# Delta-rule attention, Mish MoE and Sinkhorn MoE in one kernel: block 1's triangular inverses split between VectorE and TensorE

## The chip, the cores and the metric

One core of one Trainium2 chip runs the whole kernel. The metric is device time of one execution, in microseconds. The engines are called PE (TensorE matmul), PEld (TensorE weight load), DVE (VectorE), ACT (ScalarE), POOL (GpSimd) and SP (the queue that issues DMAs).

## What is computed

```python
def _attn_ref(q, k, v, beta):                      # 4 x 8 heads, 768 tokens, head size 48
    k_n = k / (np.linalg.norm(k, axis=-1, keepdims=True) + 1e-06)
    state = np.zeros((B, H, D, D), dtype=np.float32)
    for t in range(S):
        y[:, :, t] = np.einsum('bhd,bhde->bhe', q[:, :, t], state)
        v_old = np.einsum('bhde,bhd->bhe', state, kt)
        state = state + bt[:, :, :, None] * np.einsum('bhd,bhe->bhde', kt, vt - v_old)

def _moe_ref(x, w_in, w_out):                      # 3072 tokens, 384 -> 2048 -> 384
    h = x @ w_in
    sp = np.where(h > 20.0, h, np.log1p(np.exp(np.minimum(h, 20.0))))
    return (h * np.tanh(sp)) @ w_out

def _moe2_ref(x, w_gate, w1, w2):                  # 8 experts, 384 -> 1024 -> 384
    P = np.exp(logits - logits.max())              # then 8 rounds of row and column scaling
    for e in range(E):
        out += P[:, e:e + 1] * (np.maximum(x @ w1[e], 0.0) @ w2[e])
```

## The kernel before

The 768 tokens are cut into six blocks, c = 0 to 5, of two chunks of 64 tokens. The recurrence of a chunk becomes a 64x64 triangular inverse per head. Each inverse is made from its two 32x32 diagonal triangles: DVE inverts those by elimination, all 128 triangles of a block at once, in a tile called lane that holds one triangle per partition and 32-row group; then PE joins two 32x32 triangles to 64x64. The steps for one block are: lane_in_one (L1101, a DVE transpose of the masked Gram matrices gx into lane, and a memset of the diagonal); elim_ops (30 elimination steps, each a product at L1114 and an addition at L1120); st_lane_out (L1129 and L1130, two DVE transposes into t11 and diag); st_m1 (L1157) and st_m2 (L1172), the joining matmuls of 32x32 with evacuations between them; then st_z, st_w, st_s and st_y, the chunk's own small matmuls. diag_left (L1092, ACT) copies the lower diagonal blocks to the left ahead of lane_in_one.

While that runs, PE works through the first MoE of block c: for each of U1 = 16 slices of the hidden layer m_first (L308, nine matmuls 128x512) and, two slices later, m_second (L1341, nine matmuls). They are split in three passes of high and low parts. The order is written by hand: marks s0 to s15 are the 16 steps, f1 to f4 follow them while the last m_second drain, and s16 to s23 are the eight slices of one expert of the second MoE (e_first L308, y0_second L332), which only blocks 0 and 1 run here. Tables attach the attention work of the next block to marks: what is in pe runs as matmul stages at that mark, what is in rest is called there, and each engine executes its own instructions strictly in that written order.

Block 0 differs from the later blocks: the weights of the first MoE arrive for the first time, as 64-bit numbers. Per step, ACT makes L193 and L206, DVE makes L196 and L201 (decoding the slice used two steps later), ACT rounds it to the high part (L251), and DVE subtracts for the low part (L270), after which SP stores the slice (L279) and fetches the slice four further on (L170, L174). ACT also does Mish (L1320) and the high part of the result (L1328), and DVE its low part (L1330). m_first of a step needs L251 and L270 of that slice. Into what is left of DVE's step, fill(us) puts elimination operations of block 1's inverse from a queue eq, by an assumed cost; drain_elim empties the queue.

In block 0, block 1's diag_left stands at s1 and s2, lane_in_one at s3, eliminations from s4 on, and at s17 the rest of the eliminations, the two transposes, and POOL's work for block 1. At s18, array_kept (L1567) issues eight matmuls 128x512 whose result nothing reads, then st_m1 follows, at s19 st_z, the first half of st_m2, and st_w, and so on to s22. Small matmul stages take a PSUM bank from bank().

Of the kernel before, what the change touches and what calls it, by code (L numbers as in the profile page):

```python
# [8 lines left out]
F32 = mybir.dt.float32  # L9
# [4 lines left out]
AF = mybir.ActivationFunctionType  # L14
ALU = mybir.AluOpType
AX = mybir.AxisListType
# [69 lines left out]
def delta_mish_sinkhorn_kernel(  # L86
# [740 lines left out]
    if True:  # L827
# [6 lines left out]
        gxs = [ap_p.tile([128, 4, H, CH], F32, name=f"gx{i}") for i in range(2)]  # L834
        nrms = [[ap_p.tile([128, 4 * H], F32, name=f"{n}{i}") for n in ("ss", "ne", "rn", "bn")] for i in range(2)]
        us = [[ap_p.tile([128, 2, DM], F32, name=f"us{g}{i}") for i in range(2)] for g in range(NG)]
        lane = ap_p.tile([128, 32, 32], F32, name="lane")
        t11 = ap_p.tile([128, 32, 32], F32, name="t11")
        yd = ap_p.tile([128, 4, DM], F32, name="yd")
        diag = yd.rearrange("p t d -> p (t d)")[:, 0:1024].rearrange("p (b i) -> p b i", i=32)  # L840
# [265 lines left out]
        def elim_ops(c):  # L1106
            ops = []
            for s in range(1, 31):
                n = 31 - s
                slot = [None]  # L1110

                def prod(s=s, n=n, slot=slot):
                    slot[0] = t11.rearrange("p b i -> p (b i)")[:, 0:n * s].rearrange("p (n s) -> p n s", s=s)
                    nc.vector.tensor_tensor(  # L1114
                        out=slot[0], in0=lane[:, s + 1:32, s:s + 1].to_broadcast([128, n, s]),
                        in1=lane[:, s:s + 1, 0:s].to_broadcast([128, n, s]), op=ALU.mult,
                    )
# [8 lines left out]
            return ops  # L1126

        def st_lane_out(c):
            nc.vector.transpose(out=t11.rearrange("p b i -> p i b"), in_=lane.rearrange("p t i -> p i t"))  # L1129
            nc.vector.transpose(out=diag.rearrange("p b i -> p i b"), in_=lane)  # L1130
# [259 lines left out]
        if True:  # L1390
# [146 lines left out]
            warm(2)  # L1537
            rounded(1)
            in1 = [op for _, op in lane_in_one(1)]
            ops1 = deque(elim_ops(1))  # L1540

        NU = U1 + U2
        MARKS = [f"s{f}" for f in range(U1)] + ["f1", "f2", "f3", "f4"] + [f"s{f}" for f in range(U1, NU)]
# [17 lines left out]

        carry = []

        def array_kept():
            ps = bank()
            for _ in range(8):
                mm(ps, lhsT=x1h[:, 0, 0:128], rhs=x1h[:, 0, :], start=True, stop=True)  # L1567

        def window(c):

            pe = {m: [] for m in MARKS}
# [10 lines left out]
            if c == 0:  # L1582
                for t in (2, 3):
                    pe["s2"].append(lambda t=t: st_s(0, t))
                for t in range(4):
                    rest[f"s{1 + t // 2}"].append(lambda t=t: diag_left(1, t))
                rest["s3"].append(lambda: [op() for op in in1])
                rest["s3"].append(lambda: eq.extend(ops1))
            if nxt < NBLK:
                m0, at = PLACES[c][0:2]  # L1590
                rest[MARKS[m0]].append(drain_elim)
                if c == 0:
                    rest[MARKS[m0]].append(lambda: nc.vector.memset(seed_sb, 0.0))
                rest[MARKS[m0]].append(lambda: st_lane_out(nxt))
                if c == 0:
# [8 lines left out]
                    for m, names in ((22, "--m"), (23, "zMw"), (24, "Nsy"), (25, "ZWS"), (26, "Y"), (27, "-")):  # L1604
                        for x in names:
                            at += [m, m]
                            if x == "-":
                                ch += [lambda: lambda: None] * 2
                            elif x == "m":
                                ch += [lambda hf=hf: (hf or array_kept(), m_run(st_m1(nxt, hf))[0])[1] for hf in range(2)]  # L1610
# [47 lines left out]
        if True:  # L1658
            banks[:] = [0, [A1, A1]]
            for c in range(NBLK):  # L1660
# [44 lines left out]
                for f in range(U1 + (3 if c < NE0 else 2)):  # L1705
# [39 lines left out]
                        decodes(min(U1, f + 3))  # L1745
                        begins(min(U1, f + 4))
                    if not c:
                        fill((2.0 + 1.2, 0.7, 0.0)[f - U1] if f >= U1 else 0.0 if f == 3 else 1.0)
                    elif c < NE0:
                        fill(2.9 if f < U1 else 2.0 if f < U1 + 2 else 0.5)  # L1750
                    else:
                        fill(2.6)
# [218 lines left out]
```

## Time and profile before

| | us |
|---|---|
| median of 3 runs | 2167.09 |
| lowest, highest | 2166.68, 2168.41 |
| the profiled execution | 2170.71 |
| its span, first to last instruction | 2168.9 |
| PE busy in it | 2144.8 |
| DVE, ACT, POOL busy | 1394.2, 712.9, 629.9 |
| mean granted TensorE clock, as a share of full | 0.993 |

Times in rows are counted from the first instruction of the span. Block 0's 16 steps run from about 64 us to 143 us, marks f1 to s23 of block 0 to about 220 us. The other 1950 us hold blocks 1 to 5, which the change leaves as they are, and the rest of the second MoE.

### The profile page before, as it was taken

What the parts mean: (1) busy time and instruction counts of PE and PEld (TensorE: products, weight loads), DVE (VectorE), ACT (ScalarE), POOL (GpSimd) and SP (SyncE); (2) the same over time, 40 slices, a digit from 0 to 9 for tenths busy, and PEclk for the clock granted to TensorE, in tenths of its full rate; (3) what the DMA queues carried; (4) which work ended last, traced back from release to release, by engine and by line L of the source; (5) the groups of instructions that cost most, each with busy time, mean ns of one, the idle gap of its engine ahead of it and who ended that gap; (6) DMA issues with size and microseconds to landing.
All of it is one profiled execution on the core that took longest, in us unless ns stands there. A gap on an engine that the chain in (4) does not pass through costs nothing.

```text
span 2168.9 us, 35002 instructions
## 1 busy us (share of the span) xinstructions
PE 2144.8 (99%) x14118; PEld 1771.2 (82%) x14118; DVE 1394.2 (64%) x2316; ACT 712.9 (33%) x1332; POOL 629.9 (29%) x489
## 2 busy tenths in 40 slices
PE   8999999999999999999999999999999999999999
PEld 6778878888888888888888888888888888888887
DVE  7893846566413576776777776666666666666665
ACT  7772533343334443333333311112122211121222
POOL 4214241544224466768787400001000000000000
PEclk8999999999999999999999999999999999999999
DMA  6676636463447257655545344544444354534441
GB/s 190 233 295 221 210 119 195 135 210 129 151 167 251 88 196 262 210 198 196 212 173 211 116 156 136 186 138 149 157 151 141 131 160 145 166 133 159 156 154 44
DMA packets 148993, 370.37 MB, mean 171 GB/s; under 512 B 36832, under 2 KB 76576, under 8 KB 148576
## 3 DMA queue, kind: packets, MB, share of 16 engines
q1 hardware_dynamic: 148256, 367.75, 50.2%
q8 instruction: 111, 1.82, 0.3%
q10 hardware_dynamic: 576, 0.39, 0.1%
q14 instruction: 50, 0.41, 0.1%
HBM read 274.15 MB, written 93.95 MB: 170 GB/s over the span
## 4 chain that ended last, share of the span: by engine, by line
PE 93%; DVE 3%; ACT 2%; DMA 1%; issue 1%; SPq 0%; POOL 0%; DVEq 0%; ACTq 0%
PE s L680 34%; PE b L613 32%; PE psh L308 9%; PE x L1341 8%; PE psa L1051 2%; PE y L332 1%; PE psa L1221 1%; DMA kq<-in_w_out_dram 1%; PE psa L1255 1%; PE psa L1199 1%; PE psa L1239 1%; PE psa L1172 1%; PE psa L1362 0%; PE psa L1157 0%; ACT sq L950 0%
## 5 line engine op out<-in xcount | busy, mean ns | idle before, releaser
L613 PE MATMUL b<-gx,gw 128*128 128x512 f32 x3036 | 793.5, 389 | 0.1
L620 DVE TENSOR_TENSOR gt<-b,gt 128x512 f32<-128x512 f32 x644 | 436.1, 689 | 425.8 <-PE b L613 407.6
L613 PEld LDWEIGHTS b<-gx,gw 128*128 128x128 f32 x3036 | 569.4, 188 | 119.0 <-ACT gt L622 0.8
L680 PE MATMUL s<-gh,gw 128*128 128x512 f32 x2208 | 622.4, 390 | 0.2 <-ACT gf L710 0.2
L655 ACT ACTIVATE gh<-gt 128x512 fp32r<-128x512 f32 x368 | 232.8, 633 | 942.0 <-DVE gt L649 939.6
L680 PEld LDWEIGHTS s<-gh,gw 128*128 128x128 f32 x2208 | 413.7, 188 | 86.1 <-ACT gf L710 0.8
L680 PE MATMUL s<-gl,gw 128*128 128x512 f32 x1104 | 326.7, 390 | 0.0
L649 DVE SCALAR_TENSOR_TENSOR gt<-gt,gp 128x512 f32<-128x512 f32 x336 | 277.8, 827 | 4.5
L308 PE MATMUL psh<-x,w 128*128 128x512 f32 x1008 | 263.3, 405 | 5.9 <-ACT w L251 2.5
L680 PEld LDWEIGHTS s<-gl,gw 128*128 128x128 f32 x1104 | 206.8, 188 | 42.7
L308 PEld LDWEIGHTS psh<-x,w 128*128 128x128 f32 x1008 | 187.1, 191 | 53.6 <-DVE w L270 7.6
L658 POOL TENSOR_TENSOR gl<-gt,gh 128x512 fp32r<-128x512 f32 x128 | 185.9, 1458 | 86.3 <-ACT gh L655 78.2
L658 DVE TENSOR_TENSOR gl<-gt,gh 128x512 fp32r<-128x512 f32 x240 | 164.6, 686 | 36.3 <-ACT gh L655 36.0
L553 POOL TENSOR_TENSOR gx<-gxr,gx 128x768 fp32r<-128x768 f32 x18 | 34.9, 1940 | 413.1 <-ACT gx L552 413.1
L1341 PE MATMUL x<-gh,w 128*128 128x512 f32 x576 | 150.2, 396 | 0.1
L475 POOL TENSOR_TENSOR gw<-gr,gw 128x640 fp32r<-128x640 f32 x70 | 117.5, 1681 | 83.4 <-ACT gw L494 83.4
L1330 POOL TENSOR_TENSOR gl<-x,gh 128x512 fp32r<-128x512 f32 x55 | 70.8, 1288 | 223.2 <-ACT gh L1328 214.8
L1341 PEld LDWEIGHTS x<-gh,w 128*128 128x128 f32 x576 | 105.9, 188 | 23.3 <-issue 1.4
L1322 ACT ACTIVATE x<-psh 128x512 f32<-128x512 f32 x80 | 47.7, 596 | 119.2 <-PE psh L308 114.9
L1015 POOL TENSOR_TENSOR kq<-kq,mask_sb 64x256 f32<-64x256 f32 (+1 forms) x80 | 68.3, 854 | 48.6 <-ACT kq L1010 44.4
L1341 PE MATMUL x<-gl,w 128*128 128x512 f32 x288 | 81.0, 389 | 0.0
L475 POOL TENSOR_TENSOR gw<-raw,gw 128x384 fp32r<-128x384 f32 x70 | 74.4, 1083 | 7.3 <-ACT gw L516 7.3
(208 smaller groups left out, 1953.9 us busy)
## 6 DMA issues: line engine op xcount, KB each, us to landing
gw<-wg SPq DMA_DIRECT2D x57, 1280.0 KB, 8.1
w<-wd SPq DMA_DIRECT2D x88, 768.0 KB, 4.5
gw<-wg SPq DMA_DIRECT2D x57, 768.0 KB, 5.1
wg<-gw SPq DMA_DIRECT2D x29, 1280.0 KB, 6.2
wg<-gw SPq DMA_DIRECT2D x29, 768.0 KB, 5.2
wd<-w SPq DMA_DIRECT2D x24, 768.0 KB, 6.9
gr<-in_w_dram SPq DMA_DIRECT2D x35, 384.0 KB, 3.3
raw<-in_w_dram SPq DMA_DIRECT2D x35, 384.0 KB, 3.8
```

Source lines behind the costliest of these rows:

```text
L308: mm(ps, lhsT=wi(u, pw, kc), rhs=(xh, xl)[px][:, kc, :], start=(n == 0), stop=(n == 3 * KD - 1))
L475: nc.gpsimd.tensor_tensor(out=w[:, 1, lo:hi], in0=r, in1=w[:, 0, lo:hi].bitcast(F32), op=ALU.subtract)
L613: mm(ps, lhsT=w[:, pw, i * 128:i * 128 + 128], rhs=x[:, px, j, :], start=(n == 0), stop=(n == last))
L620: add = lambda o, i: nc.vector.tensor_tensor(out=t[:, o], in0=ps, in1=t[:, i], op=ALU.add)
L649: nc.vector.scalar_tensor_tensor(out=t, in0=t, scalar=0.0, in1=pbs[u, e][:, o:o + 512], op0=ALU.max, op1=ALU.mult)
L655: nc.scalar.activation(out=h, in_=t, func=AF.Copy)
L658: return lambda: eng.tensor_tensor(out=l, in0=t, in1=h.bitcast(F32), op=ALU.subtract)
L680: mm(o[k], lhsT=w[:, pw, at:at + 128], rhs=hids[s, z][ph], start=(start and new and n == 0), stop=(end and not new and n == 2))
L1015: nc.gpsimd.tensor_tensor(out=o, in0=o, in1=mask_sb[p, None, :].to_broadcast([64, hs.stop - hs.start, CH]), op=ALU.mult)
L1322: nc.scalar.activation(out=mi_x[u % 2], in_=hps.pop(u), func=AF.Mish)
L1330: eng.tensor_tensor(out=l, in0=p, in1=h.bitcast(F32), op=ALU.subtract)
L1341: mm(x2ps[c][k], lhsT=wo(u, pw, k * 128, k * 128 + 128), rhs=(h, l)[pg], start=(f == 0 and n == 0), stop=(f == U1 - 1 and n == 2))
```

## The change

Block 1's inverse alone, the one that is made during block 0, is cut differently. DVE now inverts 16x16 triangles: lane is widened to 1056 columns so that a view lane16 holds both halves of a triangle, and elim16_ops has 14 steps instead of 30, each acting on two halves. PE joins two 16x16 triangles to 32x32 in three stages: st_16a (128 matmuls in two halves at f1 and f2), st_16b (64 matmuls at f4) and st_16c (128 matmuls, half at f4 and half at s16). The evacuations are one ACT operation that also scales by a 0/1 column (lower16), two DVE operations (upper16), and four ACT operations into diag. halves16 makes the two columns once, by two reductions on DVE. diag_left moves from s1 and s2 to one each at s5 to s8, lane_in_one from s3 to s8, and the two transposes of st_lane_out from s17 to s15. The fill times of s3, s16 and s17 change, array_kept is gone. POOL's work for block 1 and st_m1 and all behind it keep their marks.

```diff
+        def elim16_ops():
+            ops = []
+            for s in range(1, 15):
+                n = 15 - s
...
+        def st_16a(hf):
+            if hf == 0:
+                shared16["a"] = bank().rearrange("p (b i) -> p b i", i=16)
+            ps = shared16["a"]
+            for b in range(16 * hf, 16 * hf + 16):
+                for p in range(0, 128, 32):
+                    q = slice(p, p + 16)
+                    mm(ps[p:p + 32, b], lhsT=diag[q, b, :], rhs=t11[q, b, 0:16], start=True, stop=True)
+            return lambda: hf and nc.scalar.activation(out=e16, in_=ps, func=AF.Copy, scale=lower16)
...
+                    mm(ps[q, b], lhsT=diag[q, b, :], rhs=e16[q, b, :], start=True, stop=True)
...
+                    mm(ps[p:p + 16, b], lhsT=e16[q, b, :], rhs=diag[q, b, 16:32], start=True, stop=True)
...
-            ops1 = deque(elim_ops(1))
+            ops1 = deque(elim16_ops())
+            halves16()
...
-        def array_kept():
-            ps = bank()
-            for _ in range(8):
-                mm(ps, lhsT=x1h[:, 0, 0:128], rhs=x1h[:, 0, :], start=True, stop=True)
...
                 for t in range(4):
-                    rest[f"s{1 + t // 2}"].append(lambda t=t: diag_left(1, t))
-                rest["s3"].append(lambda: [op() for op in in1])
-                rest["s3"].append(lambda: eq.extend(ops1))
+                    rest[f"s{5 + t}"].append(lambda t=t: diag_left(1, t))
+                rest["s8"].append(lambda: [op() for op in in1])
+                rest["s8"].append(lambda: eq.extend(ops1))
+                rest["s15"].append(drain_elim)
+                rest["s15"].append(lambda: st_lane_out(1))
+                pe["f1"].append(lambda: st_16a(0))
+                pe["f2"].append(lambda: st_16a(1))
+                pe["f4"] += [st_16b, lambda: st_16c(0)]
+                pe[f"s{U1}"].append(lambda: st_16c(1))
...
-                        fill((2.0 + 1.2, 0.7, 0.0)[f - U1] if f >= U1 else 0.0 if f == 3 else 1.0)
+                        fill((2.0, 0.0, 0.0)[f - U1] if f >= U1 else 1.0)
```

The first place is DVE in the steps, around lane_in_one (STREAM_TRANSPOSE of gx into lane). Before, at steps s3 and s4:

```order
L270 TENSOR_TENSOR w_1157<-kq_138,w_1157 128x768
L1101 STREAM_TRANSPOSE lane<-gx_151 128x1024
L1102 MEMSET lane 128x32
L196 SCALAR_TENSOR_TENSOR kq_139<-kq_139 128x768
L201 SCALAR_TENSOR_TENSOR kq_139<-kq_139 128x768
L1330 TENSOR_TENSOR gl<-psh,gh 128x512
L270 TENSOR_TENSOR w_1284<-kq_139,w_1284 128x768
L196 SCALAR_TENSOR_TENSOR kq_140<-kq_140 128x768
L201 SCALAR_TENSOR_TENSOR kq_140<-kq_140 128x768
L1114 TENSOR_TENSOR t_165<-lane 128x30
L1120 TENSOR_TENSOR lane<-lane,t_165 128x30
```

With the change, DVE at steps s7, s8 and s9 (L1405 is what L1330 was, L1104 what L1101 was; L1140 and L1147 are the new eliminations):

```order
L1405 TENSOR_TENSOR gl<-psh,gh 128x512
L270 TENSOR_TENSOR w_1160<-kq_139,w_1160 128x768
L1104 STREAM_TRANSPOSE lane<-gx_151 128x1024
L1105 MEMSET lane 128x32
L196 SCALAR_TENSOR_TENSOR kq_140<-kq_140 128x768
L201 SCALAR_TENSOR_TENSOR kq_140<-kq_140 128x768
L1140 TENSOR_TENSOR t_167<-lane 128x28
L1147 TENSOR_TENSOR lane<-lane,t_167 128x2x14
L1140 TENSOR_TENSOR t_167<-lane 128x52
L1147 TENSOR_TENSOR lane<-lane,t_167 128x2x13x2
L1140 TENSOR_TENSOR t_167<-lane 128x72
L1405 TENSOR_TENSOR gl<-psh,gh 128x512
```

The transpose into lane moved five steps later, steps s3 to s7 have no elimination work, and the eliminations start right behind the transpose, four or five to a step.

The second place is DVE at the end of the eliminations and the transposes out of lane (STREAM_TRANSPOSE into t and yd). Before, at s17 and s18:

```order
L1114 TENSOR_TENSOR t_165<-lane 128x30
L1120 TENSOR_TENSOR lane<-lane,t_165 128x30
L1593 MEMSET seed_sb 128x1
L1129 STREAM_TRANSPOSE t_165<-lane 128x32x32
L1130 STREAM_TRANSPOSE yd<-lane 128x32x32
L270 TENSOR_TENSOR w_91<-raw,w_91 128x768
L323 SCALAR_TENSOR_TENSOR hl<-psh,hh 128x512
L907 COPY mb_177<-psa 32x512 x2
```

With the change, at s14, s15 and f1 (the w_1161 and w_1280 slices are the first two of the expert):

```order
L1405 TENSOR_TENSOR gl<-psh,gh 128x512
L270 TENSOR_TENSOR w_1160<-kq_141,w_1160 128x768
L1147 TENSOR_TENSOR lane<-lane,t_167 128x2x2x13
L1140 TENSOR_TENSOR t_167<-lane 128x28
L1147 TENSOR_TENSOR lane<-lane,t_167 128x2x14
L270 TENSOR_TENSOR w_1161<-raw,w_1161 128x768
L1405 TENSOR_TENSOR gl<-psh,gh 128x512
L1204 STREAM_TRANSPOSE t_167<-lane 128x32x32
L1205 STREAM_TRANSPOSE yd<-lane 128x32x32
L270 TENSOR_TENSOR w_1280<-raw,w_1280 128x768
L1405 TENSOR_TENSOR gl<-psh,gh 128x512
```

The transposes now stand behind the low part (gl) of slice 14 and ahead of that of slice 15.

The third place is PE between two m_second, here of slices 13 and 14. Before:

```order
L1341 MATMUL x_1248<-gl,w_90 128x512
L1341 MATMUL x_1249<-gl,w_90 128x512
L1341 MATMUL x_1250<-gl,w_90 128x512
L1341 MATMUL x_1248<-gh,w_91 128x512
L1341 MATMUL x_1249<-gh,w_91 128x512
```

With the change, at f1 and f2 (st_16a is L1169 and reads t and yd; L1416 is what L1341 was):

```order
L1416 MATMUL x_1246<-gl,w_90 128x512
L1169 MATMUL psa<-t_167,yd 32x16 x64
L1416 MATMUL x_1244<-gh,w_91 128x512
L1416 MATMUL x_1245<-gh,w_91 128x512
L1416 MATMUL x_1246<-gh,w_91 128x512
L1416 MATMUL x_1244<-gh,w_91 128x512
L1416 MATMUL x_1245<-gh,w_91 128x512
L1416 MATMUL x_1246<-gh,w_91 128x512
L1416 MATMUL x_1244<-gl,w_91 128x512
L1416 MATMUL x_1245<-gl,w_91 128x512
L1416 MATMUL x_1246<-gl,w_91 128x512
L1169 MATMUL psa<-t_167,yd 32x16 x64
```

Between m_second of slice 13 and that of slice 14, PE now has 64 matmuls that need both transposes, and 64 more ahead of m_second of slice 15; st_16b and st_16c (192 matmuls) follow behind that one.

## Rows read from the trace of the kernel before

**Rows 1.** The page, part 4: the chain that ended last, by engine.

```profile
PE 93%; DVE 3%; ACT 2%; DMA 1%; issue 1%; SPq 0%; POOL 0%; DVEq 0%; ACTq 0%
```

**Rows 2.** Busy time by stretch: length, engines' busy us (instructions), clock, DMA share, GB/s.

```profile
100.00:120.00 20.00, 19.83 (x84) 15.16 (x83) 19.39 (x33) 16.30 (x23) 0.00 (x0) 1.00 0.98 362
...
360.00:460.00 100.00, 100.00 (x1212) 82.59 (x1211) 62.96 (x117) 37.82 (x71) 45.72 (x41) 1.00 0.54 172
```

**Rows 3.** Timeline of PE: start, length, engine, line, tiles, shape, count [idle before <-releaser].

```profile
74.00 2.32 PE L308 MATMUL psh<-x,w 128*128 128x512 f32 x9
...
83.10 0.51 PE L308 MATMUL psh<-x,w 128*128 128x512 f32 x1 [0.66 <-ACT w L251]
...
107.45 2.41 PE L308 MATMUL psh<-x,w 128*128 128x512 f32 x9
...
134.31 0.39 PE L308 MATMUL psh<-x,w 128*128 128x512 f32 x1
...
238.81 2.20 PE L308 MATMUL psh<-x,w 128*128 128x512 f32 x9
...
242.89 2.20 PE L308 MATMUL psh<-x,w 128*128 128x512 f32 x9
```

**Rows 4.** Timeline of DVE, one step of block 0.

```profile
101.81 0.69 DVE L1330 TENSOR_TENSOR gl<-psh,gh 128x512 fp32r<-128x512 f32 x1
102.42 0.95 DVE L270 TENSOR_TENSOR w<-kq,w 128x768 fp32r<-128x768 f32 x1
...
105.15 0.32 DVE L1114 TENSOR_TENSOR t<-lane 128x168 f32<-128x168 f32 x1
...
106.15 0.68 DVE L1330 TENSOR_TENSOR gl<-psh,gh 128x512 fp32r<-128x512 f32 x1
```

**Rows 5.** Timeline of DVE: transpose into lane, an elimination, the transposes out.

```profile
83.96 2.05 DVE L1101 STREAM_TRANSPOSE lane<-gx 128x1024 f32<-128x1024 f32 x1
...
96.53 0.27 DVE L1114 TENSOR_TENSOR t<-lane 128x108 f32<-128x108 f32 x1
...
152.89 2.27 DVE L1129 STREAM_TRANSPOSE t<-lane 128x1024 f32<-128x1024 f32 x1
154.98 2.04 DVE L1130 STREAM_TRANSPOSE yd<-lane 128x1024 f32<-128x1024 f32 x1
```

**Rows 6.** Timeline of ACT: diag_left, and the ends of one step.

```profile
71.64 1.70 ACT L1092 ACTIVATE gx<-gx 32x256 f32<-32x256 f32 x4
...
96.38 0.90 ACT L251 ACTIVATE w<-kq 128x768 fp32r<-128x768 f32 x1 [0.88 <-DVE kq L201]
...
99.41 0.60 ACT L1328 ACTIVATE gh<-psh 128x512 fp32r<-128x512 f32 x1
```

**Rows 7.** Timeline of PE behind the 16 steps: s16, array_kept, st_m1, st_z, s19.

```profile
143.32 2.59 PE L308 MATMUL psh<-x,w 128*128 128x512 f32 x9 [0.24 <-ACT x L1348]
...
154.12 2.01 PE L1567 MATMUL psa<-x 128*128 128x512 f32 x8
156.06 2.21 PE L1157 MATMUL psa<-t,gx 32*32 32x32 f32 x128
158.55 0.25 PE L1199 MATMUL psa<-us,kq 48*64 48x48 f32 x1 [0.28 <-ACT mb L1145]
...
160.47 0.23 PE L1199 MATMUL psa<-us,kq 48*64 48x48 f32 x1 [0.79 <-DVE mb L907]
...
161.70 3.71 PE L308 MATMUL psh<-x,w 128*128 128x512 f32 x9
```

**Rows 8.** Busy time by short stretch, columns as in rows 2.

```profile
58.00:60.00 2.00, 2.00 (x72) 1.95 (x68) 1.87 (x5) 1.36 (x3) 1.92 (x3) 1.00 0.00 0
...
66.00:68.00 2.00, 1.00 (x5) 0.51 (x3) 1.04 (x3) 1.07 (x2) 0.00 (x0) 1.00 1.04 326
...
70.00:72.00 2.00, 2.00 (x6) 1.32 (x5) 1.63 (x3) 1.83 (x3) 0.00 (x0) 0.50 1.04 424
...
162.00:163.00 1.00, 1.00 (x3) 0.81 (x3) 0.97 (x3) 0.41 (x1) 1.00 (x1) 0.50 1.07 449
```

More of the change, by code (lines that the diff above doesn't have):

```diff
@@ L836, in delta_mish_sinkhorn_kernel @@
         us = [[ap_p.tile([128, 2, DM], F32, name=f"us{g}{i}") for i in range(2)] for g in range(NG)]
-        lane = ap_p.tile([128, 32, 32], F32, name="lane")
+        lanes = ap_p.tile([128, 1056], F32, name="lane")
+        lane = lanes[:, 0:1024].rearrange("p (t i) -> p t i", i=32)
+        lane16 = lanes.rearrange("p (b x) -> p b x", b=2)[:, :, 0:512].rearrange("p b (t i) -> p b t i", i=32)
+        lower16, upper16 = [ap_p.tile([128, 1], F32, name=f"h{i}") for i in range(2)]
         t11 = ap_p.tile([128, 32, 32], F32, name="t11")
@@ L1126, in elim_ops, with prod, add @@
             return ops
+        def elim16_ops():
+            ops = []
+            for s in range(1, 15):
+                n = 15 - s
+                slot = [None]
+                def prod(s=s, n=n, slot=slot):
+                    v = t11.rearrange("p b i -> p (b i)")[:, 0:2 * n * s]
+                    slot[0] = v.rearrange("p (b n s) -> p b n s", b=2, s=s)
+                    nc.vector.tensor_tensor(
+                        out=slot[0], in0=lane16[:, :, s + 1:16, s:s + 1].to_broadcast([128, 2, n, s]),
+                        in1=lane16[:, :, s:s + 1, 0:s].to_broadcast([128, 2, n, s]), op=ALU.mult,
+                    )
+                def add(s=s, n=n, slot=slot):
+                    o = lane16[:, :, s + 1:16, 0:s]
+                    nc.vector.tensor_tensor(out=o, in0=o, in1=slot[0], op=ALU.add)
+                cost = 0.2 + 2 * n * s / 960.0
+                ops += [(cost, prod), (cost, add)]
+            return ops
@@ new lines, in halves16 @@
+        def halves16():
+            v = id_sb.rearrange("p (q h x) -> p h q x", h=2, x=16)
+            for h, o in ((0, upper16), (1, lower16)):
+                nc.vector.tensor_reduce(out=o, in_=v[:, h], axis=AX.XY, op=ALU.add)
+        e16 = mi_s[0].rearrange("p (b i) -> p b i", i=16)
+        shared16 = {}
+        def st_16a(hf):
[7 more added lines that the diff above has]
+            return lambda: hf and nc.scalar.activation(out=e16, in_=ps, func=AF.Copy, scale=lower16)
@@ new lines, in st_16b, with post @@
+        def st_16b():
+            ps = bank().rearrange("p (b i) -> p b i", i=16)
+            for b in range(32):
+                for p in (0, 64):
+                    q = slice(p, p + 32)
+                    mm(ps[q, b], lhsT=diag[q, b, :], rhs=e16[q, b, :], start=True, stop=True)
+            def post():
+                for p in (0, 64):
+                    o = t11[p:p + 32, :, 0:16]
+                    nc.vector.scalar_tensor_tensor(
+                        out=o, in0=o, scalar=upper16[p:p + 32], in1=ps[p:p + 32], op0=ALU.mult, op1=ALU.add
+                    )
+            return post
@@ new lines, in st_16c, with post @@
+        def st_16c(hf):
+            if hf == 0:
+                shared16["c"] = bank().rearrange("p (b i) -> p b i", i=16)
+            ps = shared16["c"]
+            for b in range(16 * hf, 16 * hf + 16):
+                for p in range(0, 128, 32):
+                    q = slice(p, p + 32)
+                    mm(ps[p:p + 16, b], lhsT=e16[q, b, :], rhs=diag[q, b, 16:32], start=True, stop=True)
+            def post():
+                for p in range(0, 128 * hf, 32):
+                    nc.scalar.activation(out=diag[p:p + 16, :, 16:32], in_=ps[p:p + 16], func=AF.Copy)
+            return post
@@ L1585, in window @@
                 for t in range(4):
-                    rest[f"s{1 + t // 2}"].append(lambda t=t: diag_left(1, t))
-                rest["s3"].append(lambda: [op() for op in in1])
-                rest["s3"].append(lambda: eq.extend(ops1))
+                    rest[f"s{5 + t}"].append(lambda t=t: diag_left(1, t))
[7 more added lines that the diff above has]
+                pe[f"s{U1}"].append(lambda: st_16c(1))
             if nxt < NBLK:
                 m0, at = PLACES[c][0:2]
-                rest[MARKS[m0]].append(drain_elim)
+                if c:
+                    rest[MARKS[m0]].append(drain_elim)
+                    rest[MARKS[m0]].append(lambda: st_lane_out(nxt))
                 if c == 0:
                     rest[MARKS[m0]].append(lambda: nc.vector.memset(seed_sb, 0.0))
-                rest[MARKS[m0]].append(lambda: st_lane_out(nxt))
-                if c == 0:
                     rest[MARKS[m0]].append(lambda: nc.gpsimd.memset(seed_sb, 0.0))
@@ L1609, in window @@
                             elif x == "m":
-                                ch += [lambda hf=hf: (hf or array_kept(), m_run(st_m1(nxt, hf))[0])[1] for hf in range(2)]
+                                ch += [lambda hf=hf: m_run(st_m1(nxt, hf))[0] for hf in range(2)]
                             elif x in "MN":
```

## Prediction

> **What bounds the kernel now.** I read the chain of work that ended last first: PE holds 93% of it [rows 1]. Whatever the change saves elsewhere counts only where PE waits for it. The busy times by stretch then show two regimes [rows 2]. From 360 to 460 us PE is busy all the time and DVE 63% of it: nothing done for DVE there would help. From 100 to 120 us, inside block 0's 16 steps, DVE is busy 19.39 of 20 us, and the DMA engines are at a share of 0.98. The timeline of PE says what that costs [rows 3]. Undisturbed, in block 1, m_first starts every 4.08 us (238.81 to 242.89), which is 18 matmuls of 0.227 us. In block 0 it starts at 74.00 (s2), 107.45 (s9) and 134.31 (s15): 33.45 us for the seven steps from s2, where PE's own pace would need 7 x 4.08 = 28.6, and 26.86 us, 4.48 a step, for the six from s9. One step of DVE shows why [rows 4]: from gl at 101.81 to gl at 106.15 are 4.34 us, of which 1.00 (105.15 to 106.15) are eliminations and 3.34 decoding, splitting and gl. So in this stretch DVE's step is longer than PE's, and without eliminations it would be shorter. This is the only place where the change can win, and its prize is bounded: 4.9 us from s2 to s9 and 26.9 - 24.5 = 2.4 us from s9 to s15, 7.3 us or 0.34% of the time.
>
> **Part 1, the steps s2 to s15.** In s2 to s7 the change takes everything of the inverse off DVE (3.34 us a step against PE's 4.08) and diag_left off ACT at s1 and s2, where it holds up L251 and so m_first at 83.10 [rows 3, 6]. I take PE's pace from s2 to s9: -4.9 us.
> Then the work comes back. ACT has 3.63 us a step, from L251 at 96.38 to the end of gh at 100.01, and diag_left is 1.70 for two calls, so 0.85 each [rows 6]: 4.48 us a step in s5 to s8, more than PE's 4.08. Since DVE's L270 and gl both wait for ACT, DVE cannot run ahead of PE there, and no lead is left at s8. At s8 the transpose into lane (2.05 us [rows 5]) has nothing to hide it. The 28 eliminations of 28 to 112 columns cost about what the 108-column row shows, 0.27 each [rows 5], 7.6 us in all instead of 60 operations, but they are spread over seven steps, s8 to s14, so 1.1 us a step as now. From s9 to s15 I therefore take today's 26.86 plus 2.05. s15 starts at 74.00 + 28.56 + 26.86 + 2.05 = 131.5 instead of 134.31: **-2.8 us**, with bounds of 0 (the wide loads, already at a DMA share of 0.98, land later when steps are shorter) and -4.9 (the transpose is hidden).
>
> **Part 2, the wait at f1.** The transposes out of lane move from s17 to s15, and the first half of st_16a needs both. Counted from the end of L270 of slice 15, which is what m_first of s15 waits for, DVE still has three eliminations (0.8), L270 of the expert's first slice (0.95), gl of slice 14 (0.61) and the two transposes (152.89 to 157.02, 4.13): 6.5 us [rows 4, 5]. PE has eight matmuls of m_first and nine of m_second: 17 x 0.227 = 3.9 us. The order on PE is fixed, so behind this wait stand m_second of slices 14 and 15, x2_done and all of s16. **+2.6 us**; each us by which DVE leads PE at s15 takes one off, so the bounds are 0 and 2.6, and 0 goes with the -4.9 above. Before, the transposes were covered by m_second, m_first and array_kept.
>
> **Part 3, the joining stages.** No row has a matmul of 16 columns. The nearest is st_m1: 128 matmuls 32x32 in 2.21 us, 17.3 ns each [rows 7]; by columns the new ones could cost half, 8.7. I take 17.3, because the 32x32 ones already show little of their columns. st_16a: 128 x 17.3 ns = **+2.2 us**. st_16b and st_16c: 192 x 17.3 ns = 3.3 us, of which they hide the wait of s16 for x2_done, 0.24 idle and 2.59 - 2.20 = 0.39 in the stretched m_first [rows 7]: **+2.7 us**. Bounds for the 320: 2.8 and 5.5 us. [...]
> The evacuations are one ACT operation on 512 columns, two of DVE and four of ACT. They stand behind m_second of slice 15 on engines that the eliminations have left, and I cost them at nothing; if the logits of s16 or the bank of s18 wait for them, up to 1 us. halves16, two reductions at s1, lies where DVE waits for ACT: nothing. SP's queue changes only through the times of L270.
>
> **Part 4, s18 and s19.** array_kept goes: 154.12 to 156.06, **-1.9 us**; st_m1 no longer waits for the transposes, whose results are then finished. st_z waits 0.28 and 0.79 us for the evacuations of st_m1 [rows 7]; the second is behind DVE's backlog from the transposes, so about half of both goes: **-0.5 us**. POOL's work for block 1 keeps its mark.
>
> **Part 5, the clock.** The granted clock was 0.50 at 70 to 72 us, after a stretch (66 to 68) in which PE was busy 1.00 of 2.00 us, and 0.50 at 162 to 163, after the waits of st_z [rows 8]. At 58 to 60 us, 72 small matmuls without gaps, it was 1.00. [...] What a fall costs is seen at s19: m_first took 3.71 instead of 2.20, 1.5 us [rows 3, 7]. The 2.6 us wait at f1 should bring one (+1.5); the waits of st_z shrink, so the one at s19 should not come (-1.5). I take **0**, with bounds of -1.5 and +3.0.
>
> **The sum.** -2.8 + 2.6 + 2.2 + 2.7 - 1.9 - 0.5 + 0 = +2.3 us. The profiled execution (2170.71 us, span 2168.9) would become 2173.0. The runs' median lies 3.6 us under that execution; the same difference put on it, 2167.09 + 2.3, gives **2169.4 us**. A difference of 0.2%, 4.3 us, is about what a measurement of this kernel can tell from no change, so this forecast is no change, on the slow side.
>
> **Rivals.**
> *The clock falls more often (slower).* The wait at f1 brings a fall, st_16b and st_16c (3.3 us of 16-column work without filler) a second one at s16, and the one at s19 stays because st_m1 and st_z now follow without array_kept. +2.3 + 1.5 + 1.5 = +5.3: 2172.4 us. For it: the fillers and st_z's small matmuls stand just where the clock fell. Against: 58 to 60 us [rows 8]. It decides over 0.2% once two falls come on top. Chance 0.24.
> *DVE keeps a lead (faster).* If ACT's diag_left fits into its gaps, the transpose into lane is hidden, s15 comes 4.9 us earlier, and the wait at f1 shrinks by 2.05 to about 0.6, without a fall of the clock: -4.9 + 0.6 + 2.2 + 2.7 - 1.9 - 0.5 - 1.5 = -3.3: 2163.8 us. For it: 3.34 against 4.08 on DVE. Against: 4.48 on ACT and the DMA share. Chance 0.13, about half of it beyond 0.2%.
> *16-column matmuls cost half.* -2.8 on the forecast: 2166.6 us. This is also the case that the change gives back just what it takes. Chance 0.08.
> *A floor per matmul above that of st_m1.* St_m1's two row groups alternate; if the new stages' matmuls overlap less, a matmul costs up to twice 17.3 ns. At the middle, 26 ns, the 320 take 8.3 instead of 5.5 us, +5.1 in all: 2172.2 us. Chance 0.05. [...]
>
> **How the numbers follow.** The forecast has the remaining 0.50. Faster by over 0.2% (under 2162.8): half of the second rival, 0.07. Slower by over 0.2% (over 2171.4): the first and the last, 0.29. Same: 0.64. The range runs from the second rival's time to a little over the first's, 2163.5 to 2173.5; the forecast's own bounds (part 3 at half price, part 5 at its ends) lie inside.
>
> **What the profile of the changed kernel would show.** m_first at s9 near 102.6 us and at s15 near 131.5 (part 1); a gap of PE of about 2.6 us ahead of the first st_16a, ended by a DVE transpose (part 2); st_16a, b and c at 17 ns a matmul (part 3); st_m1 right behind y0_second (part 4); a clock of 0.50 shortly behind f1 and none at s19 (part 5). I am wrong if DVE idles for PE in s9 to s15, if no gap stands at f1, or if the stretch behind s16 has more or fewer slow windows than one in place of the one at s19.

## The result, and the profile after

The changed kernel takes 2180.86 us (median of 6 runs, 2177.39 to 2185.39) against 2167.74 (6 runs, 2166.68 to 2169.77): a ratio of 1.0063 with a 95% interval of 1.0050 to 1.0075, 13 us slower. The forecast was 2169.4 us and no change, the range ended at 2173.5: it was wrong, on the side that it had called slow. One of the six executions of the small matmuls alone, below, took 3395.26 us at a granted clock of 0.585; it counts in that run's median, not in its ratio.

The profiled execution is the slowest of the six: 2185.39 us, span 2183.6, 14.7 more than before. Its page says that PE is busier by 5.9 us (before 2144.8) and that q8, a DMA queue that carries instructions, moved 116 packets (before 111).

```profile
PE 2150.7 (98%) x14750; PEld 1777.0 (81%) x14750; DVE 1383.4 (63%) x2288; ACT 715.8 (33%) x1337; POOL 629.5 (29%) x489
...
q8 instruction: 116, 1.90, 0.3%
...
PE 94%; DVE 3%; ACT 1%; issue 1%; DMA 1%; SPq 0%; DVEq 0%; ACTq 0%
```

The chain of work that ended last reads much as before [rows 1]; the loss has to be found by place. The timeline of PE from s15 to s19 answers to [rows 7] (start, length, engine, line, shape, count, idle time before and its releaser; st_16a is L1169, st_16b L1177, st_16c L1195, st_m1 L1232):

```profile
137.55 2.39 PE L308 MATMUL psh<-x,w 128*128 128x512 f32 x9
...
143.84 1.33 PE L1169 MATMUL psa<-t,yd 16*32 16x16 f32 x128 [1.86 <-DVE yd L1205]
...
148.82 1.26 PE L1169 MATMUL psa<-t,yd 16*32 16x16 f32 x128
...
152.29 2.16 PE L1177 MATMUL psa<-s,yd 32*32 32x16 f32 x125
...
156.53 1.26 PE L1195 MATMUL psa<-yd,s 32*16 32x16 f32 x128 [1.74 <-issue]
160.26 0.96 PE L1195 MATMUL psa<-yd,s 32*16 32x16 f32 x92 [2.47 <-issue]
161.15 4.21 PE L308 MATMUL psh<-x,w 128*128 128x512 f32 x9
...
172.90 2.21 PE L1232 MATMUL psa<-t,gx 32*32 32x32 f32 x128
...
177.77 2.32 PE L308 MATMUL psh<-x,w 128*128 128x512 f32 x9
```

Three things are to be seen. At f1 stands the wait for the transposes that I expected, 1.86 us. In st_16c PE stood idle for 1.74 and 2.47 us, and the releaser is "issue": nothing that the profile follows held it back. And m_first of s16 took 4.21 us instead of some 2.3. The busy time by stretch (length; PE, PEld, DVE, ACT and POOL busy with their counts; granted clock, DMA share, GB/s) explains the last of these: the clock is at 0.50 of full speed around f1 and again from before 156 until 165 us.

```profile
145.00:148.00 3.00, 3.00 (x19) 2.38 (x12) 0.07 (x1) 0.00 (x0) 0.00 (x0) 0.50 0.45 118
156.00:161.00 5.00, 2.00 (x217) 1.90 (x219) 2.19 (x3) 0.00 (x0) 0.00 (x0) 0.50 0.54 195
161.00:165.00 4.00, 4.00 (x34) 3.19 (x22) 0.00 (x0) 3.67 (x13) 0.00 (x0) 0.50 0.16 59
```

Stretch by stretch, by the starts of m_first on PE (us; "again" is the second profile of the same kernel, "left out" and "late pieces" are experiments below):

| stretch | before | after | again | joins left out | late pieces |
|---|---|---|---|---|---|
| start to s2 | 74.00 | 77.98 | 74.56 | 74.29 | 72.53 |
| s2 to s9 | 33.45 | 30.71 | 29.24 | 29.26 | 35.84 |
| s9 to s15 | 26.86 | 28.86 | 29.01 | 29.18 | 29.20 |
| s15 to s16 | 9.01 | 23.60 | 24.55 | 8.60 | 13.11 |
| s16 to s19 | 18.38 | 16.62 | 16.86 | 15.76 | 17.97 |
| s19 to s21 | 25.96 | 23.96 | 21.21 | 24.99 | 23.75 |
| s21 to the end | 1981.2 | 1981.9 | 1982.1 | 1982.2 | 1981.9 |
| span | 2168.9 | 2183.6 | 2177.5 | 2164.3 | 2174.3 |

The loss is one stretch, s15 to s16, where the joining stages stand: 14.6 and 15.5 us.

### The profile page after: what moved, and what is told of

Same layout as the page of the kernel before. It is cut to its first block, busy times and chain, and to the rows that moved or that the text cites. A ratio compares the mean times of both kernels' runs of the same rounds, so it can differ in the third digit from the quotient of the medians.

```text
span 2183.6 us, 36250 instructions
## 1 busy us (share of the span) xinstructions
PE 2150.7 (98%) x14750; PEld 1777.0 (81%) x14750; DVE 1383.4 (63%) x2288; ACT 715.8 (33%) x1337; POOL 629.5 (29%) x489
## 4 chain that ended last, share of the span: by engine, by line
PE 94%; DVE 3%; ACT 1%; issue 1%; DMA 1%; SPq 0%; DVEq 0%; ACTq 0%
PE s L680 34%; PE b L613 31%; PE psh L308 9%; PE x L1416 8%; PE psa L1054 2%; PE y L332 2%; PE psa L1296 1%; PE psa L1330 1%; PE psa L1274 1%; PE psa L1247 1%; PE psa L1232 1%; PE psa L1314 1%; PE psa L1437 1%; PE spare L1451 1%; DMA kq<-in_qkb_dram 0%
## 5 line engine op out<-in xcount | busy, mean ns | idle before, releaser
L1416 PE MATMUL x<-gh,w 128*128 128x512 f32 x576 | 151.7, 399 | 0.1
L1405 POOL TENSOR_TENSOR gl<-x,gh 128x512 fp32r<-128x512 f32 x55 | 70.7, 1285 | 224.2 <-ACT gh L1403 215.6
L1416 PEld LDWEIGHTS x<-gh,w 128*128 128x128 f32 x576 | 106.5, 189 | 23.4 <-issue 1.4
L1416 PE MATMUL x<-gl,w 128*128 128x512 f32 x288 | 81.3, 390 | 0.0
```

The source lines that it names most:

```text
L1405: eng.tensor_tensor(out=l, in0=p, in1=h.bitcast(F32), op=ALU.subtract)
L1416: mm(x2ps[c][k], lhsT=wo(u, pw, k * 128, k * 128 + 128), rhs=(h, l)[pg], start=(f == 0 and n == 0), stop=(f == U1 - 1 and n == 2))
```

## Experiments

Theory A: **instruction supply**. Each joining matmul, on 32-bit data, shows in the trace as two matmul records with a weight load each, so it is four PE instructions, and 320 of them 1280. The theory has them come in q8's packets, of 16,384 bytes each: there are 116 packets for 29,500 records of PE (matmuls and weight loads) and 111 for the 28,236 before, one for every 256, rounded up. Between the two gaps of st_16c lie exactly 128 matmul records with 128 weight loads, 256 instructions. The timeline shows PE using those up in 1.26 us. Rivals: the small matmuls cost what they cost wherever they stand (B), the clock is the loss (C), or the moved DVE work or the missing fillers are (D). Each kernel below was timed together with the kernel before; ratios are to that.

**The changed kernel again** (no edit).

> The changed kernel once more, unaltered. Its first profile reached s2 4.0 us later than the kernel before (77.98 against 74.00), in code that the change leaves as it is, with the clock at 0.50 for 23.9 us ahead of s0 instead of 13.7. If that is chance: s2 comes at another time in this profile, and the median stays 11 to 13 us over before, from the stretch s15 to s16 (23.60 us against 9.01). If it belongs to the change: s2 is at 77 to 79 us again.

2179.31 us against 2168.55, ratio 1.0051 (1.0036 to 1.0066). s2 came at 74.56, so the late start of the first profile does not belong to every execution. The same gaps stand in st_16c:

```profile
L1169 PE MATMUL psa<-t,yd 16*32 16x16 f32 x256 | 3.2, 195 | 1.9 <-DVE yd L1205 1.9
...
L1177 PE MATMUL psa<-s,yd 32*32 32x16 f32 x128 | 2.2, 178 | 0.0
L1195 PE MATMUL psa<-yd,s 32*16 32x16 f32 x256 | 2.7, 186 | 3.9 <-issue 3.9
```

These are groups by line: busy time, mean ns of one (st_16a's 195 ns against 1.25 us for 128 of them, so not its price), idle time before them and what ended it.

**The joins left out.** The 320 matmuls and their evacuations are missing, so block 1's inverses stay unjoined.

```
-                pe["f1"].append(lambda: st_16a(0))
-                pe["f2"].append(lambda: st_16a(1))
-                pe["f4"] += [st_16b, lambda: st_16c(0)]
-                pe[f"s{U1}"].append(lambda: st_16c(1))
```

> The changed kernel with the three joining stages left out (320 matmuls and their evacuations; block 1's inverses then stay unjoined). Theory 'the joins': everything lost lies in s15 to s16: wait at f1 1.9, st_16a 2.6, st_16b 2.1, st_16c 2.7, idle time in st_16c 4.2, slower dense matmuls at half clock about 3.5, together 17 of which 0.6 was hidden; s15 to s16 comes down from 23.6 to 8 to 10 us, the clock stays 1.00 there, and the whole is 2164 to 2168 us, no slower than before. Rival 'the moved DVE work or the lost filler': 5 us or more remain over before, 2172 us or more.

2166.07 us, ratio 0.9985 (0.9976 to 0.9994). This settles D: taken together, the moved DVE work and the missing fillers lose nothing, and the loss comes with the joins. It also says what the rest of the change is worth: with joins for nothing the kernel would win 2.5 us by the medians. Between 130 and 215 us one gap of 0.3 us or more without a releaser is left, in st_m2 (L1247), which the change does not touch:

```profile
169.00 1.22 PE L1247 MATMUL psa<-yd,mb 32*32 32x32 f32 x46 [2.74 <-issue]
```

**The joins spread.** st_16c's halves stand behind m_first of s16 and of s17.

```
-                pe["f4"] += [st_16b, lambda: st_16c(0)]
-                pe[f"s{U1}"].append(lambda: st_16c(1))
+                pe["f4"].append(st_16b)
+                pe[f"s{U1}"] += [idle, idle, lambda: st_16c(0)]
+                pe[f"s{U1 + 1}"] += [idle, idle, lambda: st_16c(1)]
```

> The changed kernel with the same 320 matmuls, but st_16c's halves no longer behind st_16b: one behind m_first of s16, one behind m_first of s17. Theory 'instruction supply': PE idles in st_16c for 1.74 and 2.47 us with no releaser because 256 small instructions are used up faster than the next piece arrives; nine 128x512 matmuls between the pieces give it time. The two gaps go (4.2 us), with them the fall of the clock at 155 us (about 2 us): 2173 to 2176 us. Rival 'the small matmuls themselves, or the clock falls anyway': 2179 to 2182 us as now.

2180.46 us, ratio 1.0058 (1.0045 to 1.0071): what B and C said. The gaps shrank, but they did not vanish (timeline of PE):

```profile
158.10 1.30 PE L1195 MATMUL psa<-yd,s 32*16 32x16 f32 x128 [1.04 <-DVE t L1182]
...
163.44 1.19 PE L1195 MATMUL psa<-yd,s 32*16 32x16 f32 x124 [1.05 <-issue]
...
167.17 1.22 PE L308 MATMUL psh<-x,w 128*128 128x512 f32 x2 [0.81 <-issue]
...
189.90 0.80 PE L1247 MATMUL psa<-yd,mb 32*32 32x32 f32 x23 [3.17 <-issue]
```

The gaps of st_16c, 1.74 and 2.47 us in the first profile, are 1.05 and 0.81 here, and the second stands in the middle of a large m_first, so such a gap is not a property of st_16c. The 3.17 us in st_m2 can't be charged to the joins, since 2.74 us stand there without them. A's expectation of the size was wrong: nine large matmuls were not enough relief. The gaps that did go bought no time either; PE waited 1.04 us for DVE instead, and two stretches of 6.8 us at half clock followed, at 165 and 189 us. What each of these cost was not separated.

**The small matmuls alone.** Put into the kernel before, at the same places, on a constant tile.

```
+                    mm(ps[o, b], lhsT=id_sb[q, m], rhs=id_sb[q, k], start=True, stop=True)
+                pe["f1"].append(lambda: small16("a", 0))
+                pe["f2"].append(lambda: small16("a", 1))
+                pe["f4"] += [lambda: small16("b", 0), lambda: small16("c", 0)]
+                pe[f"s{U1}"].append(lambda: small16("c", 1))
```

> The kernel before with 320 small matmuls of the same shapes on a constant tile at the same places (f1, f2, f4, s16), waiting for nothing and read by nobody: the disputed cost by itself. By my prediction's price (17.3 ns each, some hidden) 4.9 to 5.5 us: 2172 to 2174. By 'instruction supply' (2.6 + 2.1 + 2.7 for the matmuls, 4.2 for the gaps, 0 to 3 for the clock, 0.6 hidden) 11 to 14 us: 2178 to 2182, with gaps without a releaser behind every 128 matmul records.

2185.76 us, ratio 1.0079 (1.0064 to 1.0094), over A's range and three times my price. Without any wait for data PE idles 5.5 us, always 256 instructions or a multiple apart:

```profile
144.07 0.88 PE L1138 MATMUL psa<-id_sb 16*32 16x16 f32 x83 [0.74 <-issue]
...
152.61 1.25 PE L1138 MATMUL psa<-id_sb 32*16 32x16 f32 x128 [1.48 <-issue]
157.16 0.95 PE L1138 MATMUL psa<-id_sb 32*16 32x16 f32 x92 [3.30 <-issue]
```

**The same, 20 a step.** From s0 to s15, between the large groups.

```
+                for f in range(U1):
+                    for kind in "abc":
+                        pe[f"s{f}"].append(lambda f=f, kind=kind: small16(kind, range(2 * f, 2 * f + 2)))
```

> The kernel before with the same kinds of small matmuls as in the run that put 320 of them at f1, f2, f4 and s16 (17.2 us by the medians, 54 ns each), now 20 in each step s0 to s15 (12 in s2, 312 in all), between the nine-matmul groups 128x512. Theory 'instruction supply': 20 small ones and 18 large ones are some 116 PE instructions in a step of over 4 us, less than the 256 that took 3.73 us behind one fetch, so no idle time without a releaser; cost is at most 312 x 20 ns = 6.2 us and less where PE waits for DVE anyway (s9 to s15): 2169 to 2175 us. Rival 'a small matmul costs 54 ns wherever it stands': 2183 to 2187 us.

2181.87 us, ratio 1.0065 (1.0050 to 1.0080), between the two expectations. The trace shows two reasons. In s2 the small matmuls' PSUM bank waited for DVE, an accident of the place, and a stretch at half clock followed (m_second took 4.14 us there, 2.27 in later steps): that step took 11.56 us (73.19 to 84.75). From s4 on no gap and no wait is left, and every step takes 5.10 us where 18 large matmuls take 4.08 [rows 3]:

```profile
79.73 0.40 PE L1138 MATMUL psa<-id_sb 32*32 32x16 f32 x8 [3.96 <-DVE us L907]
...
94.73 0.43 PE L1138 MATMUL psa<-id_sb 16*32 16x16 f32 x24
95.09 2.33 PE L308 MATMUL psh<-x,w 128*128 128x512 f32 x9
97.35 0.28 PE L1138 MATMUL psa<-id_sb 32*16 32x16 f32 x16
97.56 1.65 PE L1354 MATMUL x<-gh,w 128*128 128x512 f32 x6
99.06 0.84 PE L1354 MATMUL x<-gl,w 128*128 128x512 f32 x3
99.83 0.34 PE L1138 MATMUL psa<-id_sb 16*32 16x16 f32 x18
```

Read by starts, 24 and 16 small records take 0.36 and 0.21 us, 0.57 in all; nine large matmuls take 2.26 and 2.27 behind them instead of 2.04, 0.22 more each time. So 1.02 us for 20, 51 ns each, without a single gap: A is right that the gaps need density, and B is right that the price stays high, since each change to large matmuls costs about as much as one of them, 0.22 against 0.227 us. A change here is a place where PE goes from the small matmuls to a group of nine large ones. From s3 to s15 only 5.2 us of the 12.2 came through (61.34 us against 56.11), because PE waits for DVE there anyway.

**Half the instructions.** As "alone", in half precision: one matmul record and one weight load each.

```
-                    mm(ps[o, b], lhsT=id_sb[q, m], rhs=id_sb[q, k], start=True, stop=True)
+                    mm(ps[o, b], lhsT=id_r[q, m], rhs=id_r[q, k], start=True, stop=True)
```

> The kernel before with the 320 small matmuls on a constant tile at f1, f2, f4 and s16, as in the run that took 17.2 us more than before, but in half precision: one matmul record and one weight load for each instead of two and two, so 640 PE instructions instead of 1280. Theory 'what counts is instructions, their start and their supply': 3.2 us for the matmuls, 0.7 for the changes to large ones, 1 to 3 of idle time, 0 to 3 for the clock: 2173 to 2178. Rival 'a small product costs what it costs, whatever its passes': 2183 to 2187.

2176.8 us, ratio 1.0041 (1.0029 to 1.0053), inside A's range: 8.8 us instead of 17.2 for the same 320 products. In the small stages one gap is left, behind 164 records, and a record still costs some 9 ns (0.57 us from start to start for the first 64).

```profile
145.08 1.75 PE L1139 MATMUL psa<-id_r 32*32 32x16 f16 x164
148.77 0.33 PE L1139 MATMUL psa<-id_r 32*16 32x16 f16 x28 [1.94 <-issue]
```

**No wait at f1.** st_16a works on a constant tile.

```
-                    mm(ps[p:p + 32, b], lhsT=diag[q, b, :], rhs=t11[q, b, 0:16], start=True, stop=True)
+                    mm(ps[p:p + 32, b], lhsT=id_sb[q, 0:32], rhs=id_sb[q, 0:16], start=True, stop=True)
```

> The changed kernel with st_16a working on a constant tile instead of the transposes' results (its product is then not the one wanted; all else as it was): the wait of PE at f1, 1.86 us, goes alone. If the first fall of the clock is due to that wait: -1.9 - 2.3, 2175 to 2177 us. If the clock falls behind f1 all the same, as it did with 320 small matmuls that wait for nothing: -1.9 at most, 2177 to 2180.

2180.39 us, ratio 1.0062 (1.0049 to 1.0075): nothing gained, just over the range for a clock that falls all the same. The wait is gone and four gaps, 6.1 us in all, stand where two, 3.9 us in all, were in the second profile (4.2 in the first):

```profile
141.34 0.88 PE L1169 MATMUL psa<-id_sb 16*32 16x16 f32 x83 [0.67 <-issue]
...
146.16 1.93 PE L1177 MATMUL psa<-s,yd 32*32 32x16 f32 x88 [1.01 <-issue]
...
149.89 1.25 PE L1195 MATMUL psa<-yd,s 32*16 32x16 f32 x128 [1.38 <-issue]
154.17 0.95 PE L1195 MATMUL psa<-yd,s 32*16 32x16 f32 x92 [3.03 <-issue]
```

PE came earlier and only stood longer without a releaser: in this stretch 256 instructions took 3.7 to 4.8 us from resume to resume. The wait that I had put at 2.6 us was real, 1.86 us, and taking it away gained nothing.

**Dense matmuls in the idle time.** 37 matmuls 128x384 that nobody reads: 12 ahead of st_16a, 10 ahead of st_16c, 5 behind each of its first three quarters.

```
+                dense(12, U1 - 1, True)
...
+            dense(10 if hf == 0 else 5, U1, hf == 0)
...
+                    if p == 0 and b % 16 == 8:
+                        dense(5, U1)
```

> The changed kernel with matmuls 128x384 that nobody reads where PE stood idle: 12 (some 2.0 us) ahead of st_16a at f1, where it waited 1.86 us, and 25 (some 4 us) between the four quarters of st_16c, where it idled 3.9 us without a releaser. They add no more work than there was idle time. Theory 'the clock is a cost of its own': the two falls of the clock (6.8 and 10.2 us at 0.50 in the second profile of the changed kernel, 3.7 us of added time by its dense matmuls) follow the idling and go with it: 2175 to 2178 us. Rival 'the clock falls there anyway, or the fillers add to the gaps': 2180 to 2185.

2182.22 us, ratio 1.0072 (1.0060 to 1.0084): the rival's number. The trace shows both halves of it. The clock did in part what C said: it was at 0.50 from 151.0 to 154.4 us and twice more for 3.4 us, at 175 and 189 us, 10.2 us in all against 17.1 in the second profile of the changed kernel. But the fillers took 9.0 us (2.27 + 2.69 + 1.71 + 1.15 + 1.14), and 1.3 us of gaps remained; I had priced them at 6.0, without the 0.2 us at each change and the slow stretch. So the clock's share of the loss is not priced by this run.

```profile
151.00:154.40 3.40, 3.40 (x74) 2.92 (x73) 1.69 (x3) 0.00 (x0) 0.00 (x0) 0.50 0.54 181
154.40:159.00 4.60, 4.44 (x204) 3.50 (x202) 0.00 (x0) 0.00 (x0) 0.00 (x0) 1.00 0.33 129
```

**The inverse moved forward.** diag_left at s1 to s4, lane_in_one and the eliminations from s4, the transposes at s11 and s12, the joins in pieces of 32 between s13 and s16.

```
+                rest["s11"].append(lambda: st_lane_out(1, 0))
+                rest["s12"].append(lambda: st_lane_out(1, 1))
+                pe["s13"] += [a[0], no, a[1]]
+                pe["s14"] += [a[2], no, a[3]]
+                pe["s15"] += [no, no, b[0]]
```

> The changed kernel with its inverse moved forward: diag_left one each at s1 to s4, lane_in_one and the eliminations from s4, one transpose out of lane at s11 and one at s12, and the 320 joining matmuls in pieces of 32 between s13 and s16. Theory 'instruction supply': no gap without a releaser in the joining stages, no wait at f1, at most one more stretch at half clock than with the joins left out (2166.1); 320 x 20 ns = 6.3 us, and 0 to 3 us for the transposes in the steps: 2171 to 2176 us. Rival 'a joining matmul costs 41 ns wherever it stands' (13.2 us over the run without joins): 2179 us or more.

2184.72 us, ratio 1.0075 (1.0061 to 1.0089): far over A's range, in that of the rival. The joining stages had no gap, as A said, but the first piece at s13 waited for DVE, the clock was at 0.50 from there on for 10 us, and m_first of s18 waited 2.14 us for DVE's low part.

```profile
128.40 1.05 PE L1169 MATMUL psa<-t,yd 16*32 16x16 f32 x64 [3.43 <-DVE yd L1209]
```

**Late pieces.** The same, with the pieces from s14 to s17.

```
-                pe["s13"] += [a[0], no, a[1]]
-                pe["s14"] += [a[2], no, a[3]]
+                pe["s14"] += [a[0], no, a[1]]
+                pe["s15"] += [a[2], no, a[3]]
...
+                pe["s16"] += [no, no, c3[2]]
+                pe["s17"] += [no, no, c3[3]]
```

> The run with the inverse moved forward (transposes out of lane at s11 and s12), but its joining pieces one step later, from s14 to s17, so that none waits for DVE (3.43 us there at s13, and 2.14 at s18). If the loss is the sum of parts that were read (320 matmuls at 20 ns 6.3 us, some ten changes to large matmuls at 0.22 us 2.2 us, transposes in the steps 1.5 us, over 2166.1 with the joins left out) and no idle time or fall of the clock is added: 2175 to 2177. If transposes or evacuations again make PE wait over 2 us and the clock falls for it: 2179 to 2184.

2176.72 us, ratio 1.0041 (1.0029 to 1.0053), inside the range of the sum of parts. From 134 to 160 us PE is busy for all 26.00 us at a clock of 1.00, without a wait or a gap:

```profile
134.00:160.00 26.00, 26.00 (x663) 21.30 (x663) 11.35 (x18) 17.07 (x68) 2.62 (x5) 1.00 0.48 162
```

So 2 to 4 us of the loss (8.7 over before instead of 10.8 and 13.1) are gaps, waits and clock that a better order takes back, and the rest stays.

**array_kept put back, and taken out of the kernel before.** Two runs on the same eight fillers (the first lines in the changed kernel, the last in the kernel before).

```
+                                ch += [lambda hf=hf: (hf or array_kept(), m_run(st_m1(nxt, hf))[0])[1] for hf in range(2)]
...
-                                ch += [lambda hf=hf: (hf or array_kept(), m_run(st_m1(nxt, hf))[0])[1] for hf in range(2)]
```

> The changed kernel with array_kept (eight matmuls 128x512, read by nobody) put back ahead of st_m1. By my sum its removal is worth 1.9 us: 2181 to 2182.5. If the fillers keep the clock up behind them or give the next instructions time to arrive, they cost less: 2177 to 2180, with no clock of 0.50 and a shorter gap without a releaser at st_m2.

> The kernel before without array_kept, the one part that was to win on its own. By my sum -1.9 us: 2166 to 2167. If its time comes back as a longer gap at st_m2 (0.82 us before) or as a wait for the transposes ahead of st_m1: 2168 to 2170.

Put back into the changed kernel, they give 2184.09, ratio 1.0070 (1.0057 to 1.0082): 15.3 us over before instead of 10.8 and 13.1, with intervals that overlap. By the medians they cost what they last, 1.9 us, or more; the intervals do not settle it. Taken out of the kernel before, 2169.79 against 2168.8, ratio 1.0010 (1.0001 to 1.0020): no gain, rather 1 us lost. There st_m1 waits for the transposes that array_kept had covered, and 16 us at half clock follow:

```profile
157.33 2.21 PE L1157 MATMUL psa<-t,gx 32*32 32x32 f32 x128 [0.92 <-DVE t L1129]
```

The same kernel's busy time behind that, with the clock as the third number from the end:

```profile
160.00:176.00 16.00, 15.15 (x161) 13.54 (x161) 5.24 (x9) 6.16 (x11) 12.02 (x6) 0.50 0.90 318
```

No kernel of these beats the kernel before but the one that leaves the joins out.

**One reading across all traces.** If a gap with releaser "issue" is a wait for instructions, it must end a fixed time behind an instruction packet. Between 130 and 215 us, 13 of the 14 traces have such gaps of 0.3 us or more, 33 in all. Every one ends 2.2 to 2.9 us after the start of the last packet of q8 before it: in the first profile of the changed kernel packets start at 154.12 and 157.65, and PE resumes at 156.53 and 160.26. The queue moves little meanwhile (q8 from 150 to 162 us: packets, MB, share of 16 engines), so what PE waits for looks like latency rather than bandwidth:

```profile
q8 instruction: 4, 0.07, 2.2%
```

From resume to resume that is 3.73 us for 256 instructions (156.53 to 160.26; 152.75 to 156.48 in the second profile), against the 1.26 us in which PE executes them.

The same traces can be counted instead of timed. I number PE's matmul records from 0 at the start of the program. The first records behind the two gaps of st_16c are 1869 and 1997 in both profiles of the changed kernel, and in all 33 gaps the number divided by 128 leaves a remainder of 70 to 77. With its weight load a record is two instructions, so every gap stands at nearly the same place of a block of 256, whatever stage the kernel has there. This ties the gaps to the packets more firmly than the times do. The gap in st_m2 is the same: 14 x 128 + 72 before, 19 x 128 + 72 after. What changes its length, from 0.31 to 3.17 us, no run shows.

## Why the prediction was wrong

The step that failed is **part 3**, the joining stages, in its price and in what it left out. In the first profile s15 to s21 grew by 10.8 us (53.35 to 64.18) where my terms made +5.1:

| term, s15 to s21 | forecast | measured |
|---|---|---|
| 320 matmuls, with the changes to large ones | +4.9 | +7.8 |
| gaps without a releaser | 0 | +5.1 |
| wait at f1 | +2.6 | +1.9 |
| clock | 0 | +1.7 |
| array_kept, waits of st_z | -2.4 | -2.5 |
| the rest: other waits and stretched rows of before | 0 | -3.2 |

The measured 7.8 are the three stages from start to start without their idle time, 7.1 us (2.45 for st_16a, 2.02 for st_16b, 2.63 for st_16c), and three changes at 0.22. The gaps are 1.74 + 2.47 here and 1.67 at st_m2, less the 0.82 that the kernel before has there. The clock is the time by which large matmuls were stretched, 4.9 us after and 3.2 before. The last line is what remains to 10.8; most of it is two things that the kernel before has and this trace has not: waits of 0.15, 0.24 and 0.62 us at s15, s16 and s18, and st_s of s20 at half clock (2.73 us against 1.57).

*The gaps* were a term that I did not have, and the trace of before had one to show: st_m2 idles 0.82 us with releaser "issue".

```profile
171.78 0.31 PE L1172 MATMUL psa<-yd,mb 32*32 32x32 f32 x9 [0.39 <-DVE us L907]
172.91 1.07 PE L1172 MATMUL psa<-yd,mb 32*32 32x32 f32 x55 [0.82 <-issue]
```

I passed over it because no instruction could be blamed, and so put these waits at nothing without a reason. What the traces show of them is 16,384 bytes a packet and 256 instructions between the gaps of st_16c. With 20 small matmuls a step between the 128x512 ones no gap came from s4 to s15; with 320 of them at f1, f2, f4 and s16 the gaps were up to 3.30 us.

*The price.* I read st_m1's "x128" as 128 matmuls of the program; it is 64, with two records each [rows 7]. So 17.3 ns was the price of a record, and I multiplied it by 320 where there are 640. A record of st_16a and st_16c costs some 10 ns (1.26 us for 128 is 9.8), close to what I had called half price; one of st_16b, which has st_m1's 32x32 weights and half its columns, costs 15.8. The two mistakes partly cancelled, and my upper bound of 5.5 us was still under the 7.1 that came. The change back to large matmuls, 0.22 us each, was missing.

**Part 1 was right in its mechanism**, and up to 2.1 us off in its size. From s2 to s9 I said -4.9: -4.2 in the second profile (-2.7 in the first). From s9 to s15 I said 2.05 more than before, the transpose into lane: +2.15 and +2.0, and m_first of s10 waits 1.80 us behind it. The sum of -2.8 came out as -2.1 and -0.7.

**Part 2** had the right place and a size inside its bounds, and no weight: without the wait, gaps stood in its stead and the time was the same.

**Part 4** was right on st_z (waits of 0.5 us instead of 1.07) and on s19, where the clock stayed at 1.00. The -1.9 for array_kept held in the changed kernel, but not by itself: taken out of the kernel before it gained nothing.

**Part 5.** A fall behind f1 came as foretold. The second, at s16, belonged to my first rival, *the clock falls more often*; it had the right sign and place, but its 1.5 us a fall came from a short stretch (3.4 us, from 161.3 us in the kernel before), while this one lasted 10 us and began at 155.1 us, during the first of the two gaps. With 2172.4 us that rival fell short by 8.5.

**The chances.** Slower by over 0.2% had 0.29. That the sum had a side on which nothing bounded it, since PE's instructions were counted nowhere, was the reason for too narrow a range. The prize was bounded at 7.3 us; leaving the joins out shows 2.5, less than the 7.1 us of their bare matmuls. No order that was tried won. An order that puts the joins where PE waits for DVE anyway is not excluded, since there 5.2 of 12.2 us came through (the run with 20 a step).

**What stays open.** The second profile is 8.6 us over before, the medians 10.8 and 13.1: the rest differs from execution to execution, and I did not follow it. The late start (s2 at 77.98, and 77.74 in the joins spread) came in two of the nine profiles of kernels made from the changed one and in none of the five made from the kernel before, with 23.9 and 27.3 us at 0.50 ahead of s0 (before 13.7); whether the timed runs have it more often than the kernel before was not measured. How far ahead of PE its instructions are brought, and why PE resumes no sooner than 2.2 us behind the start of a packet, no run shows.

## What to carry to other kernels

Count PE's instructions, not only its busy time: each small 32-bit matmul was four instructions here (two matmul records, two weight loads), and 256 instructions took 1.26 us to execute and 3.73 us from resume to resume. A gap with releaser "issue" beside small matmuls in the profile is a warning that more of them there can cost over twice their busy time (the small matmuls alone cost 17.2 us and kept PE busy for 7.7), and that taking away a wait ahead of them may only lengthen the gaps (from 3.9 to 6.1 us without the wait at f1). Before moving work from an engine with slack to the one that sets the end, run the kernel with the new work left out: if that gains less than the bare time of the new work, it can win only where the new work fills time in which the engine waits anyway.

## What the runs showed of the hardware that was not expected

- PE stood idle in what reads as waits for instructions: 33 gaps in 13 of 14 traces, each ending 2.2 to 2.9 us after an instruction packet started and each at nearly the same place of a block of 256 instructions (the number of the first record behind it, divided by 128, leaves 70 to 77); 3.73 us at the shortest from one gap's end to the next for 256 instructions, while the same kinds of matmuls 20 a step showed no gap from s4 to s15.
- A change from small to 128x512 matmuls cost 0.22 us, nine of them taking 2.26 instead of 2.04 us.
- Small products in half precision, one record instead of two, cost half: 8.8 instead of 17.2 us for 320.
- The clock fell to 0.50 of full speed during the first of st_16c's gaps and stayed there for 10 us; with large matmuls in them the time at 0.50 from f1 to s21 went from 17.1 to 10.2 us, at no gain in time.
